# Batch 2's second MLP product: a third quad of half-size products, and four products of each quad added alone

## The chip, the core and the metric

The kernel runs on one core of a Trainium2 chip. Its engines run side by side and each works through its own instructions in order: TensorE (PE) multiplies matrices into PSUM, ScalarE (ACT) and VectorE (DVE) read PSUM and write SBUF, GpSimd (POOL) works on SBUF and issues many of the loads, SyncE (SP) issues the stores and the transposing DMAs. Semaphores hold an instruction back until what it reads is written and what it overwrites has been read. The metric is the device time of one run in microseconds, smaller being better.

## The reference

Block-sparse attention over 4 batches, 8 heads, 768 tokens and 64 columns a head, and then a residual MLP block of width 512 on the result:

```python
scores = (q @ k^T) / 8, masked by blocks of 32      # attn = softmax(scores) @ v
x  = attn, heads side by side                       # 4 x 768 x 512
u  = x + lam * (w_tok @ (alpha1 * x + beta1))       # mixes tokens
a2 = alpha2 * u + beta2
out = u + lam * (relu(a2 @ w_ch1) @ w_ch2)          # 512 -> 2048 -> 512
```

The last line has the first MLP product (to 2048 hidden columns), the relu, and the second MLP product (back to 512 columns). The change is in how the second product of batch 2 is computed.

## The kernel before

The 16 pairs of heads (four in each batch) go through attention one after the other; each pair has nine units of 128 keys by up to 512 queries for both key blocks. For a unit PE makes the scores (line 605), ACT the exponential (623), DVE multiplies by the mask (640, `emit_keep`), PE multiplies by the values (675), and at the end of a head DVE divides by the sums (692, 693). POOL, for a few heads DVE, then forms `alpha1 * x + beta1` (709, 710, `emit_a1pp`). When two pairs are through, PE mixes their tokens (`job_tok2`, 850), DVE adds the result to x (862), and transposing DMAs on SP's queue (`emit_udma`) turn it for the MLP. When a batch is complete its MLP follows, woven into the attention of the next batch.

The first MLP product of a batch is 32 jobs (`job_f1`, 923): each makes 128 hidden columns for 384 tokens (half c of the batch) with four matmuls, and ACT writes the relu (930). The second product works on six tiles of 128 tokens. In batches 0 and 1 a tile takes four "g" jobs (`job_f2`, 1075), each of four matmuls of 512 columns, into one PSUM tile, and one add of 512 columns by DVE (1084). In batch 3 and, for some tiles, in batch 2, tiles t and t + 3 are taken together as a quad: a 2 x 2 block product in which seven half-size products (eight matmuls of 256 columns each, `job_p` and `mul`, 1189) stand for eight. For that DVE first forms sums of blocks of the weights (`job_t`) and, for every quad, four sums of hidden blocks ("S" jobs, `job_s`, 1162); afterwards it adds the products into x (`plus`, 1199). In batch 2, tiles 0 and 3 are done straight with eight g jobs, and t = 1, 2 are quads. In a quad of the version before, products 1, 6 and 5 pile up in one PSUM tile and 7 and 4 in another, and DVE adds the tile after each. The last batch has its first product in a similar form: "M" jobs (`job_m`, 1036), for which sums of weights ("W" jobs, `job_w`, 986) and of inputs ("D" jobs, `job_d`, 1001) are formed by DVE.

Nothing is reordered by a planner: the order in which instructions are issued is the order on each engine. For the first 45 units it comes from `PLAN`: a job stands at unit int(when), before or after that unit's other work, by the fraction (`fns`). After that it comes from the strings W1, W2, W2L and W3. Each string of the first three is a third of a pair, and each letter a job, taken from the front of its list: q scores of three units and the first exponential, x an exponential, k a masking multiply, p a block of the value product, f a first-product job, g a second-product job (the quads' products too), T token mixing, S a sum for a quad, W and D the sums for the last batch, a the a1pp of pair 15's first head, d a transposing DMA, Y, K, Q, L copies and loads. The strings of W2L (lines 69 to 80) hold pairs 12 to 15; W3 (83 to 86) the rest.

[...] A first-product job, a token-mixing job, a third of the score tiles, a straight tile and most half-size products each take an "mm" tile. Each new one gets the buffer that was given back first, and its first matmul waits until the engine that empties that buffer is done:

```python
def mm_tile(shape=(P, DM), dt=FP):
    return psum.tile(list(shape), dt, name="mm", tag="mm", bufs=3)
```

Of the kernel before, what the change touches and what calls it, by code (L numbers as in the profile page):

```python
# [66 lines left out]
]  # L67
W2L = [
# [12 lines left out]
]  # L81
W3 = [
# [4 lines left out]
]  # L87
STR = (2, 3)
HN = NH // 2
HC = DM // 2  # L90
FW = 6
FIRST = [
    (0, 1), (0, 2), (1, 1), (1, 2), (0, 6), (2, 1), (1, 6), (2, 2), (0, 5), (0, 7),
    (1, 5), (1, 7), (0, 3), (2, 6), (1, 3), (0, 4), None, None, None, (1, 4),
# [65 lines left out]
    "tok0_1": 16.29,  # L160
    "tok0_2": 17.09,
    "tok0_3": 18.68,
    "loadq4": 18.7,
    "lv3": 19.01,
    "loadk4": 19.19,
    "tok0_4": 19.61,
    "mask5": 20.08,
    "mask9": 20.29,
    "tq3": 20.7,
    "tok0_5": 20.76,  # L170
    "loadv5": 20.77,
    "loadq5": 21.09,
    "tk3": 22.44,
    "loadk5": 22.78,
    "udma0": 23.28,
# [77 lines left out]
def kernel(  # L253
# [211 lines left out]
    def sp_tile():  # L465
        return psum.tile([P, 2, 512], FP, name="sp", tag="sp", bufs=2)
# [6 lines left out]
    def mm_tile(shape=(P, DM), dt=FP):  # L473
        return psum.tile(list(shape), dt, name="mm", tag="mm", bufs=3)

    def op_tile(shape):
        phase["op"] += 1
        if phase["first"] and phase["op"] % 2 == 0:
            return mm_tile(shape)
        return psum.tile(shape, FP, name="op", tag="op", bufs=1)  # L480
# [434 lines left out]
    def h_row(b, c, n):  # L915
        if (b, c) not in hts:
            hts[(b, c)] = ap_.tile([P, NH, QC], BF, name="hts", tag="hts", bufs=2)
        return hts[(b, c)][:, n, :]

    def job_f1(b, c, n):  # L920
        ps = mm_tile()
        for dk in range(4):
            nc.tensor.matmul(  # L923
                ps[:, 0:QC],
                w1b[:, dk, ts(n, P)],
                uTs[b][:, dk, ts(c, QC)],
                start=(dk == 0),
                stop=(dk == 3),
            )
        nc.scalar.activation(h_row(b, c, n), ps[:, 0:QC], AF.Relu)  # L930
        did.add(("f", b, c, n))

    wsum, usum = [], []
# [194 lines left out]
    )  # L1128

    xs = {}  # L1130

    def a_of(b, t, name, r=slice(0, HN)):
        if name in ("X1", "X2"):
            return xs[(b, t, name)][:, r]
        c, half = {"11": (0, 0), "12": (0, 1), "21": (1, 0), "22": (1, 1)}[name]
        return hts[(b, c)][:, HN * half + r.start : HN * half + r.stop, ts(t, P)]

# [7 lines left out]
    def job_s(b, t, n, r=slice(0, HN)):  # L1145
        dst, a, c, op = SOP[n]
        relu_late()
        rows = range(r.start, r.stop)
        for name in (a, c):
            if name[0] == "X":  # L1150
                assert all(("S", b, t, int(name[1]), m) in did for m in rows)
            else:
                h, half = divmod(int(name) - 11, 10)
                assert all(("f", b, h, HN * half + m) in did for m in rows)
        if n == 3:
            assert all(("S", b, t, 1, m) in did for m in rows)
        if n == 4:
            assert (b, t, 2) in did
        if dst[0] == "X" and (b, t, dst) not in xs:
            tag, bufs = ("eT", 6) if b == B - 1 else ("xs", 4)  # L1160
            xs[(b, t, dst)] = ap_.tile([P, HN, P], BF, name="xs", tag=tag, bufs=bufs)
        nc.vector.tensor_tensor(
            out=a_of(b, t, dst, r), in0=a_of(b, t, a, r), in1=a_of(b, t, c, r), op=op
        )
        did.update(("S", b, t, n, m) for m in rows)
# [12 lines left out]
    def mul(b, t, n, ps, start, cols=slice(0, HC), rows=slice(0, HN)):  # L1178
        a, m, need = PROD[n]
        assert m in bq or all((m, r) in did for r in range(0, HN, 2))  # L1180
        if need:
            assert all(("S", b, t, need, r) in did for r in range(HN))
        ends = (0, HN - 1)
        c, half = {"1": (0, 0), "X": (1, 0)}.get(a[0], (1, 0))
        if need == 0:
            h, half = divmod(int(a) - 11, 10)
            assert all(("f", b, h, HN * half + r) in did for r in range(rows.start, rows.stop))
        for r in range(rows.start, rows.stop):
            nc.tensor.matmul(  # L1189
                ps,  # L1190
                a_of(b, t, a)[:, r],
                b_rows(m, r)[:, 0, cols],
                start=(start and r == ends[0]),
                stop=(r == ends[1]),
                skip_group_check=True,
            )
# [4 lines left out]
    def twice(ps):  # L1201
        return ps.unsqueeze(1).broadcast_to([P, 2, HC])

    lo, hi = slice(0, HC), slice(HC, DM)

    def job_p(b, t, n, rows=slice(0, HN)):
        x = x_sbs[b]
# [86 lines left out]
    def start_mlp(b):  # L1294
        if b == B - 1:
            todo["f"] += [
                lambda j=j: job_m(*j) if len(j) == 2 else job_f1(*j) for j in last_f1()
            ]
        else:
            todo["f"] += [  # L1300
                lambda c=c, n=n: job_f1(b, c, n) for c in range(2) for n in range(NH)
            ]
        if b not in STR:
            todo["g"] += [
                lambda o=o, g=g: job_f2(b, o, g) for o in range(NT) for g in range(4)
            ]
            return
        todo["g"] += [
            lambda j=j: job_f2(b, *j[:2]) if j[-1] == "g" else job_p(b, *j)
            for j in P_ORDER[b]  # L1310
        ]
        todo["S"] += [lambda t=t, n=n, r=r: job_s(b, t, n, r) for t, n, r in S_ORDER[b]]

    REST = (6, 7, 5, 4, 3)
    P_ORDER = {
        2: [(0, g, "g") for g in range(4)]
        + [(t, 2) for t in (1, 2)]
        + [(3, g, "g") for g in range(4)]
        + [(t, 1) for t in (1, 2)]
        + [(t, n) for t in (1, 2) for n in REST],  # L1320
        3: [(0, 1, slice(r, r + 2)) for r in (0, 2, 4)]
        + [(1, 1), (0, 1, slice(6, HN)), (2, 1)]
        + [(t, 2) for t in range(2)]
        + [(t, n) for t in range(2) for n in REST]
        + [(2, n) for n in (2,) + REST],
    }
    ALL, R1, R2 = slice(0, HN), slice(0, HN // 2), slice(HN // 2, HN)
    S_ORDER = {
        2: [(t, n, ALL) for t in (1, 2) for n in (1, 2, 3, 4)],
        3: [(0, n, r) for r in (R1, R2) for n in (1, 2)]  # L1330
        + [(0, n, ALL) for n in (3, 4)]
        + [(t, n, ALL) for t in (1, 2) for n in (1, 2, 3, 4)],
# [237 lines left out]
```

## Time and profile before

| | us |
|---|---|
| median of three runs (297.27 to 297.41) | 297.3 |
| profiled execution | 297.57 |
| its span | 295.9 |
| PE busy | 289.2 |
| DVE busy | 240.6 |
| ACT busy | 217.0 |
| POOL busy | 110.1 |

The profile is of one execution. Its page begins with each engine's busy time and its share of the span; below stand 40 slices of the span, 7.4 us each, with a digit for the busy share in tenths, 9 being 90% or more. Other views show instructions in order of time with start, duration, engine, line of the kernel, operation, what it writes from what it reads, and in brackets the idle time before it and what ended it; groups of equal instructions with their count and mean; the chain of work that ended last; and the busy time of each engine in a stretch. The ends of matmuls are modelled: their starts are what counts.

### The profile page before, as it was taken

The numbers are of one execution on the slowest core, as the hardware profiler recorded it, in microseconds if no ns is written. First come the engines' busy times: TensorE is split into PE (matmuls) and PEld (weight loads), VectorE is DVE, ScalarE is ACT, GpSimd is POOL, SyncE is SP. The second block draws the span as 40 slices with busy tenths as digits, with TensorE's granted clock in tenths as the row PEclk, the third lists the DMA queues.
The fourth block names the chain that finished last, engine by engine and source line by source line (L and its number), as shares of the span: only waits on it lengthen the run. The fifth ranks groups of instructions, "written<-read, shape, count | busy, mean of one in ns | idle before, by whom it ended". The sixth has DMA issues, their size and how long they took to land.

```text
span 295.9 us, 7583 instructions
## 1 busy us (share of the span) xinstructions
PE 289.2 (98%) x3097; PEld 192.7 (65%) x3097; DVE 240.6 (81%) x498; ACT 217.0 (73%) x324; POOL 110.1 (37%) x149
## 2 busy tenths in 40 slices
PE   7999999999999999999999999999999999999995
PEld 2678878665467565565576556465567678766884
DVE  4988899995668887988758788795946999999894
ACT  5999989999799872999779780899869764477000
POOL 8997978632343720347321450335320300000000
PEclk9999999999999999999999999999999999999999
DMA  6999999981392996737962957653520214400023
GB/s 176 204 198 167 193 158 204 177 143 27 95 143 60 106 190 103 109 75 98 122 122 57 142 77 161 91 123 44 96 62 2 53 38 20 151 1 3 0 91 124
DMA packets 57274, 31.09 MB, mean 105 GB/s; under 512 B 37204, under 2 KB 54016, under 8 KB 57240
## 3 DMA queue, kind: packets, MB, share of 16 engines
q0 software_dynamic: 16752, 14.22, 33.6%
q1 hardware_dynamic: 40020, 15.92, 28.2%
q8 instruction: 24, 0.39, 0.6%
q10 hardware_dynamic: 468, 0.47, 0.6%
q14 instruction: 10, 0.08, 0.1%
HBM read 29.75 MB, written 6.29 MB: 122 GB/s over the span
## 4 chain that ended last, share of the span: by engine, by line
PE 84%; DVE 5%; ACT 4%; DMA 4%; issue 1%; POOL 1%; POOLq 0%
PE mm L923 20%; PE mm L1075 16%; PE sp L605 8%; PE op L675 8%; PE mm L850 8%; PE mm L1189 5%; ACT eT L623 4%; PE mm L605 3%; DMA kr<-in_k_dram 3%; PE sp L1189 3%; PE sp L1036 3%; PE mm L1036 3%; PE op L652 2%; PE mm L826 2%; DVE eT L640 1%; DMA x_sb<-in_q_dram 1%
## 5 line engine op out<-in xcount | busy, mean ns | idle before, releaser
L623 ACT ACTIVATE eT<-sp,expb 128x1024 f16<-128x1024 f32 x111 | 118.4, 1118 | 2.4 <-PE sp L605 1.8
L640 DVE TENSOR_TENSOR eT<-eT,mask 128x1024 f16<-128x1024 f16 x99 | 80.1, 835 | 14.2 <-ACT eT L623 14.0
L709 POOL TENSOR_TENSOR a1pp<-x_sb,vbc 128x384 bf16<-128x384 f32 x25 | 28.5, 1139 | 119.2 <-DVE x_sb L693 84.6
L923 PE MATMUL mm<-uT,w1b 128*128 128x384 bf16 x384 | 70.6, 326 | 0.1
L623 ACT ACTIVATE eT<-mm,expb 128x512 f16<-128x512 f32 x66 | 41.7, 684 | 26.6 <-PE mm L605 26.3
L1075 PE MATMUL mm<-w2b,hts 128*128 128x512 bf16 x224 | 54.7, 380 | 0.0
L930 ACT ACTIVATE hts<-mm 128x384 bf16<-128x384 f32 x96 | 45.1, 501 | 10.1 <-PE mm L923 9.5
L923 PEld LDWEIGHTS <-w1b 128*128 128x128 bf16 x384 | 35.6, 98 | 23.9 <-issue 2.4
L675 PEld LDWEIGHTS <-eT 128*128 128x128 f16 x792 | 29.8, 98 | 8.5 <-issue 1.7
L1075 PEld LDWEIGHTS <-hts 128*128 128x128 bf16 x224 | 19.8, 98 | 22.3 <-issue 3.9
L675 PE MATMUL op<-vext,eT 128*128 128x65 f16 x792 | 32.2, 194 | 0.0
L605 PE MATMUL sp<-qTs,kTs 88*128 88x512 bf16 (+1 forms) x120 | 27.0, 325 | 1.3 <-ACT eT L623 0.7
L710 POOL TENSOR_TENSOR a1pp<-a1pp,vbc 128x384 bf16<-128x384 bf16 x25 | 26.9, 1075 | 2.0
L850 PE MATMUL mm<-a1pp,wtokT 128*128 128x256 bf16 x216 | 25.9, 273 | 0.1
L850 PEld LDWEIGHTS <-wtokT 128*128 128x128 bf16 x216 | 20.6, 98 | 5.6 <-issue 1.8
L1189 PEld LDWEIGHTS <-hts 128*128 128x128 bf16 x208 | 19.6, 98 | 3.3 <-issue 0.3
L862 DVE TENSOR_TENSOR x_sb<-x_sb,mm 128x512 f32<-128x512 f32 x18 | 12.3, 684 | 9.9 <-PE mm L850 9.8
L605 PE MATMUL sp<-qhT,khT 64*128 64x256 bf16 (+1 forms) x176 | 19.8, 322 | 0.0
L605 PEld LDWEIGHTS <-khT 64*128 64x128 bf16 x264 | 10.6, 94 | 12.7 <-issue 9.2
L652 PEld LDWEIGHTS <-eT 128*128 128x128 f16 x360 | 14.9, 98 | 3.8 <-issue 0.3
L1084 DVE TENSOR_TENSOR x_sb<-x_sb,mm 128x512 f32<-128x512 f32 x14 | 9.6, 685 | 8.8 <-PE mm L1075 8.7
L693 DVE TENSOR_TENSOR x_sb<-op,rcp 128x384 f32<-128x384 f32 x28 | 15.6, 557 | 1.0
(137 smaller groups left out, 395.2 us busy)
## 6 DMA issues: line engine op xcount, KB each, us to landing
out_dram<-x_sb SPq DMA_DIRECT2D x23, 256.0 KB
qpad<-in_q_dram POOLq DMA_DIRECT2D x15, 192.0 KB, 4.5
kr<-in_k_dram POOLq DMA_DIRECT2D x15, 192.0 KB, 5.3
vr<-in_v_dram POOLq DMA_DIRECT2D x15, 192.0 KB, 5.9
w1b<-in_moe_w_ch_dram POOLq DMA_DIRECT2D x4, 512.0 KB, 9.8
w2b<-in_moe_w_ch_dram POOLq DMA_DIRECT2D x4, 512.0 KB, 8.5
hts<-in_moe_w_tok_dram POOLq DMA_DIRECT2D x2, 576.0 KB, 8.9
x_sb<-in_k_dram ACTq DMA_DIRECT2D x2, 192.0 KB
```

The costliest lines, as they stand in the source:

```text
L605: nc.tensor.matmul(sp[jj][:, dst], lhsT, rhs, start=True, stop=True, skip_group_check=True,)
L623: nc.scalar.activation(dst, at, AF.Exp, bias=expb[:], scale=SCALE)
L640: nc.vector.tensor_mul(out=e, in0=e, in1=keep)
L652: nc.tensor.matmul(op[0][:, o, :], ets[u][:, jj, h * QB + n * P : h * QB + n * P + P], vexts[i % NVB][:, w, 2 * jp + jj, :], start=op[1] == 0,
L675: nc.tensor.matmul(op[0][:, o, :], ets[u][:, jj, h * QB + n * P : h * QB + n * P + P], vexts[i % NVB][:, w, 2 * jp + jj, :], start=op[1] == 0,
L709: eng.tensor_tensor(out=dst, in0=x_sbs[b][:, :, cols], in1=bc[0], op=ALU.mult)
L710: eng.tensor_tensor(out=dst, in0=dst, in1=bc[1], op=ALU.add)
L850: nc.tensor.matmul(ps[:, o], wtokT[:, os_, ts(2 * n + o, P)], a1pps[i][:, os_, :], start=(os_ == 0 and o == 0), stop=(os_ == NT - 1 and o ...
L923: nc.tensor.matmul(ps[:, 0:QC], w1b[:, dk, ts(n, P)], uTs[b][:, dk, ts(c, QC)], start=(dk == 0), stop=(dk == 3),)
L930: nc.scalar.activation(h_row(b, c, n), ps[:, 0:QC], AF.Relu)
L1075: nc.tensor.matmul(ps[:], ht[:, nk, ts(o % 3, P)], w2b[:, nk, :], start=(nk == 0), stop=(nk == NH - 1),)
L1189: nc.tensor.matmul(ps, a_of(b, t, a)[:, r], b_rows(m, r)[:, 0, cols], start=(start and r == ends[0]), stop=(r == ends[1]), skip_group_chec ...
```

## The change

Batch 2's second product now has three quads (t = 0, 1, 2) and no straight tile. They go through a new function, `job_pi`: products 1, 2, 4 and 7 each take an "mm" tile of their own and are added to every block of x that needs them (product 1 to all four, 7 to two); only 6, 5 and 3 pile up in one tile. Most sums are formed in two halves (R1 and R2), and the first-product jobs of the batch's second half go in the order 0, 8, 1, 9, ... so that both halves of the hidden columns grow together. The relu of one of them, (2, 1, 1), moves from ACT to DVE. Quad 2's sums lie in buffers that held keys and values. The strings are written anew to fit. In the first part the loads of queries and keys of pair 4 and of queries of pair 5 stand earlier in `PLAN`, and one transposing DMA (the second d of line 70) stands one string earlier. Cut to its core:

```diff
 W2L = [
     "q 0 p p g k x L x p f k 1 K 2 k",
-    "q Q 0 g x g f v v s T T x k 1 k p p g g T g g Y d 2 k",
-    "q g 0 k g d 1 2 p x k g x k",
+    "q Q 0 g x g f v v s T T x k 1 k p p g g T g g Y d d 2 k",
+    "q g 0 k g 1 2 p x k g x k",
     "q 0 p k x v Q v 1 2 p k x g k g",
     "q 0 p 1 g x k f K k x f p p k 2 f",
     "q k 0 f x f p s f f x 1 L p k 2 f f f k Y f",
-    "q f L f 0 f k W W W W W W W W 1 f Y x f p g x f p f g k k 2",
-    "q x k x k Q 0 g 1 s f f g p 2 p f f k p f",
-    "q T 0 k f 1 x k f T x f 2 p k K p f",
-    "q x 0 x T k 1 k f 2 k f Q f d p L",
-    "q x 0 x K k g d k s f g f 1 k p p S S g 2",
-    "q p Y x x k g k S 0 1 k 2 g v g v g",
+    "q f L f 0 f k W W W W W W W W 1 f Y x f p g x f p f g k k 2 f",
+    "q x k x k Q 0 g 1 s f p f p 2 g f f k p f",
+    "q S S S S S S T 0 k f 1 x k f T x f 2 p k K p f",
+    "q S S S S x 0 x T k 1 k f 2 k f Q f d p L",
+    "q x 0 x K k g d k s f g 1 k p p S S S S g 2",
+    "q p Y x x k g k S 0 1 k a S 2 g v g v",
 ]
 W3 = [
-    "a p p p g s g g T S T S T S S S d g g U g v g D g D D g D g D g D D",
-    "f f f W W f W W f f f f f W f f f f f W f f f f f f f W f f",
-    "W f f f f f f f f f f f f f f f S f f f f S f f f f f f f f f g f f f g f g g f",
+    "p p p g g s g g T S T S T S S d g g U g v S g D g S S D D g D D g D D",
+    "f f f f W f f W f f W f f W f f f f f f W f f f f f f f f f",
+    "f W f f f f f f f W f f f f f S f f W f f S f f f f f f f f f g f f f g f g g f",
     "g S S g g S g S g S g S g S g S g g S g S g S g g g S g g g g g",
 ]
...
+HALVES = [n // 2 + HN * (n % 2) for n in range(NH)]
+ON_DVE = [(2, 1, 1)]
...
-    "loadq4": 18.7,
+    "loadq4": 15.391,
-    "loadk4": 19.19,
+    "loadk4": 15.495,
-    "loadq5": 21.09,
+    "loadq5": 20.705,
...
-        nc.scalar.activation(h_row(b, c, n), ps[:, 0:QC], AF.Relu)
+        if (b, c, n) in ON_DVE:
+            nc.vector.tensor_scalar_max(out=h_row(b, c, n), in0=ps[:, 0:QC], scalar1=0.0)
+        else:
+            nc.scalar.activation(h_row(b, c, n), ps[:, 0:QC], AF.Relu)
...
+        if dst[0] == "X" and (b, t) == SPLIT:
+            xs[(b, t, dst, r.start // R2.start)] = ap_.tile(
+                [P, HN // 2, P], BF, name="xs", tag="kr" if n == 1 else "vr", bufs=2
+            )
...
+    def job_pi(b, t, n):
+        x = x_sbs[b]
+        quad = x[:, t : t + 4 : 3].rearrange("p a (h c) -> p a h c", h=2)
+        if n == 6:
+            banks[(b, t)] = (sp_tile()[:, 0] if t < 2 else op_tile([P, DM])[:])[:, lo]
+        chained = n in (6, 5, 3)
+        ps = banks[(b, t)] if chained else mm_tile()[:, lo]
+        mul(b, t, n, ps, n not in (5, 3))
+        if n == 1:
+            plus(quad, ps.unsqueeze(1).unsqueeze(1).broadcast_to([P, 2, 2, HC]))
+        elif n == 7:
+            plus(quad[:, 1], twice(ps))
+        else:
+            plus(quad[:, int(n in (4, 6, 5)), int(n in (3, 5))], ps)
+        did.add((b, t, n))
+        for o, uses in ((t + 3, (1, 4, 6, 7, 5)), (t, (1, 2, 5, 3))):
+            if n in uses and all((b, t, m) in did for m in uses):
+                emit_store(b, o, slice(0, DM))
...
     P_ORDER = {
-        2: [(0, g, "g") for g in range(4)]
-        + [(t, 2) for t in (1, 2)]
-        + [(3, g, "g") for g in range(4)]
-        + [(t, 1) for t in (1, 2)]
-        + [(t, n) for t in (1, 2) for n in REST],
+        2: [(0, 1), (0, 2), (1, 1), (2, 1), (1, 2), (2, 2)]
+        + [(0, 4), (1, 4), (2, 4), (0, 6), (1, 6), (0, 7), (0, 5), (1, 7)]
+        + [(1, 5), (0, 3), (2, 6), (1, 3), (2, 5), (2, 7), (2, 3)],
...
     S_ORDER = {
-        2: [(t, n, ALL) for t in (1, 2) for n in (1, 2, 3, 4)],
+        2: [(t, n, R1) for t in range(3) for n in (1, 2, 3)]
+        + [(0, 4, R1)]
+        + [(t, n, R2) for t in range(2) for n in (1, 2)]
+        + [(0, 3, R2), (1, 3, R2), (0, 4, R2)]
+        + [(1, 4, ALL), (2, 1, R2), (2, 2, R2), (2, 3, R2)]
+        + [(2, 4, r) for r in (R1, R2)],
```

More of the change, by code (lines that the diff above doesn't have):

```diff
@@ L1130 @@
     xs = {}
+    ALL, R1, R2 = slice(0, HN), slice(0, HN // 2), slice(HN // 2, HN)
+    SPLIT = (B - 2, 2)
     def a_of(b, t, name, r=slice(0, HN)):
         if name in ("X1", "X2"):
-            return xs[(b, t, name)][:, r]
+            if (b, t) != SPLIT:
+                return xs[(b, t, name)][:, r]
+            n, h = r.start // R2.start, R2.start
+            return xs[(b, t, name, n)][:, r.start - h * n : r.stop - h * n]
         c, half = {"11": (0, 0), "12": (0, 1), "21": (1, 0), "22": (1, 1)}[name]
@@ L1158, in job_s @@
             assert (b, t, 2) in did
-        if dst[0] == "X" and (b, t, dst) not in xs:
+        if dst[0] == "X" and (b, t) == SPLIT:
+            xs[(b, t, dst, r.start // R2.start)] = ap_.tile(
+                [P, HN // 2, P], BF, name="xs", tag="kr" if n == 1 else "vr", bufs=2
+            )
+        elif dst[0] == "X" and (b, t, dst) not in xs:
             tag, bufs = ("eT", 6) if b == B - 1 else ("xs", 4)
@@ L1190, in mul @@
                 ps,
-                a_of(b, t, a)[:, r],
+                a_of(b, t, a, slice(r, r + 1))[:, 0],
                 b_rows(m, r)[:, 0, cols],
@@ L1300, in start_mlp @@
             todo["f"] += [
-                lambda c=c, n=n: job_f1(b, c, n) for c in range(2) for n in range(NH)
+                lambda c=c, n=n: job_f1(b, c, n)
+                for c in range(2)
+                for n in (HALVES if b in STR and c == 1 else range(NH))
             ]
@@ L1308, in start_mlp @@
         todo["g"] += [
-            lambda j=j: job_f2(b, *j[:2]) if j[-1] == "g" else job_p(b, *j)
-            for j in P_ORDER[b]
+            lambda j=j: (job_p if b == B - 1 else job_pi)(b, *j) for j in P_ORDER[b]
         ]
@@ L1326 @@
     }
-    ALL, R1, R2 = slice(0, HN), slice(0, HN // 2), slice(HN // 2, HN)
     S_ORDER = {
-        2: [(t, n, ALL) for t in (1, 2) for n in (1, 2, 3, 4)],
+        2: [(t, n, R1) for t in range(3) for n in (1, 2, 3)]
[4 more added lines that the diff above has]
+        + [(2, 4, r) for r in (R1, R2)],
         3: [(0, n, r) for r in (R1, R2) for n in (1, 2)]
```

## The prediction

> **What bounds the kernel now.** I read the page's busy shares and slices first, then a table by stretch, then single instructions in order of time. Strings of the written order are named by their line in the kernel (line 75 is the seventh of W2L); a sum of the S jobs is a "sum", "DVE" is VectorE, "PE" TensorE, "ACT" ScalarE, "POOL" GpSimd.
>
> ```profile
> PE 289.2 (98%) x3097; PEld 192.7 (65%) x3097; DVE 240.6 (81%) x498; ACT 217.0 (73%) x324; POOL 110.1 (37%) x149
> PE   7999999999999999999999999999999999999995
> DVE  4988899995668887988758788795946999999894
> ```
>
> PE is full from end to end, so any wait put into it lengthens the run. DVE has room on average, but from slice 31 on (about 229 us) it is nearly full too. The stretches are those of the strings at lines 75 and 79, and of the last batch's first MLP product:
>
> ```profile
> 203.66:211.53 7.87, 7.87 (x69) 4.48 (x70) 6.06 (x14) 6.75 (x12) 1.97 (x3) 1.00 0.83 129
> 229.77:235.63 5.86, 5.74 (x64) 3.85 (x62) 5.61 (x10) 4.56 (x8) 2.25 (x2) 1.00 0.35 67
> 255.34:274.22 18.88, 18.88 (x121) 11.59 (x119) 18.01 (x58) 13.85 (x32) 0.00 (x0) 1.00 0.08 30
> ```
>
> After the length come PE, weight loads, DVE, ACT, POOL. The string at 75 leaves DVE 1.8 us, the one at 79 only 0.25, the long stretch 0.87 of 18.88.
>
> How can DVE hold PE up? The "mm" PSUM tile has three buffers, taken in turn. In order of time, with start and duration:
>
> ```profile
> 230.60 1.05 PE L1189 MATMUL mm<-w2b,hts 128*128 128x256 bf16 x8
> 231.48 0.81 PE L923 MATMUL mm<-uT,w1b 128*128 128x384 bf16 x4
> 231.49 1.41 DVE L640 TENSOR_TENSOR eT<-eT,mask 128x1024 f16<-128x1024 f16 x1 [0.21 <-ACT eT L623]
> 232.13 1.04 PE L1189 MATMUL mm<-w2b,hts 128*128 128x256 bf16 x8
> 232.82 0.41 DVE L1199 TENSOR_TENSOR x_sb<-x_sb,mm 128x256 f32<-128x256 f32 x1
> 233.16 1.08 DVE L640 TENSOR_TENSOR eT<-eT,mask 128x1024 f16<-128x1024 f16 x1
> 233.29 0.81 PE L923 MATMUL mm<-uT,w1b 128*128 128x384 bf16 x4
> 234.49 0.68 DVE L640 TENSOR_TENSOR eT<-eT,mask 128x1024 f16<-128x1024 f16 x1
> ```
>
> Three tiles are taken from 230.60 to 232.13; the fourth needs the first one's buffer. A product takes 0.87 (next fence), so PE was ready at 233.00; it started at 233.29, just after the add at 232.82 + 0.41 = 233.23 had emptied that buffer. The add was late because a masking multiply stood before it on DVE. This wait of 0.29 is what the change makes more of.
>
> **PE work.** From the chain of waits, start and length:
>
> ```profile
> 208.20 0.86 PE mm L1075 x4
> 213.32 1.30 PE mm L923 x8
> 222.01 1.31 PE mm L850 x12
> 253.86 1.75 PE mm L1189 x16
> ```
>
> Tiles 0 and 3 cost eight chunks of 0.86, 6.88 us; their quad costs seven products of 1.75 / 2 = 0.875, 6.12. PE saves **0.76**. A first-product job (f1) takes 0.65, a token-mixing job of the last pairs 1.31.
>
> **DVE work.** Groups by form, busy time and mean ns from 180 us on:
>
> ```profile
> L1052 DVE TENSOR_TENSOR hts<-mm,part 128x384 bf16<-128x384 f32 x24 | 13.1, 551 | 0.7 <-PE mm L1036 0.5
> L1199 DVE TENSOR_TENSOR x_sb<-x_sb,mm 128x256 f32<-128x256 f32 x15 | 6.1, 415 | 0.9 <-PE mm L1189 0.7
> L1019 DVE TENSOR_SCALAR hts<-hts 128x384 bf16<-128x384 bf16 x24 | 5.8, 249 | 0.0
> L1162 DVE TENSOR_TENSOR hts<-hts 128x1024 bf16<-128x1024 bf16 x5 | 3.4, 683 | 0.0
> L1199 DVE TENSOR_TENSOR x_sb<-x_sb,sp 128x512 f32<-128x512 f32 x4 | 2.7, 682 | 0.5 <-PE sp L1189 0.5
> L1162 DVE TENSOR_TENSOR xs<-hts 128x512 bf16<-128x512 bf16 x2 | 0.8, 421 | 0.0
> ```
>
> Product 1, added alone, goes to four blocks, 128x1024. No row has that add. Its bounds are 0.68 (the bf16 sum of that size, SBUF only) and 1.36 (two adds of 512); 415 ns at 256 and 682 at 512 give 1.04 ns an element, so 1.21 us is my estimate, from the rows of the same kind. A quad's adds come to 1.21 + 5 x 0.415 + 0.68 = 3.97; before, 6 x 0.415 + 0.68 = 3.17, and a straight pair 2 x 0.68. Three quads are 11.9 against 7.7: +4.2. The sums were 8 x 0.68 = 5.5 and become 22 x 0.42 + 0.68 = 9.9: +4.4. One relu comes from ACT: it reads PSUM, so between L1019's 0.25 and L1052's 0.55; nearer the second, which reads PSUM too, 0.5. Together DVE gets some **9 us** more, nearly all of it in the strings 75 to 80. What counts is where PE needs a buffer that DVE has not emptied.
>
> *String 75*, in order of time:
>
> ```profile
> 205.44 0.69 DVE L640 TENSOR_TENSOR eT<-eT,mask 128x1024 f16<-128x1024 f16 x1 [1.84 <-ACT eT L623]
> 206.05 1.96 DVE L986 TENSOR_TENSOR wsum<-w1b 128x768 bf16<-128x768 bf16 x4
> 208.86 1.02 DVE L986 TENSOR_TENSOR wsum<-w1b,wsum 128x768 bf16<-128x768 bf16 x2
> 209.80 0.35 DVE L333 COPY vext<-vr 128x768 f16<-128x768 f16 x1
> 210.12 0.20 DVE L692 RECIPROCAL rcp<-op 128x6 f32<-128x6 f32 x1
> 210.57 1.03 PE L1075 MATMUL mm<-w2b,hts 128*128 128x512 bf16 x4
> 210.83 2.08 DVE L640 TENSOR_TENSOR eT<-eT,mask 128x1024 f16<-128x1024 f16 x2
> 211.00 1.36 POOL L709 TENSOR_TENSOR a1pp<-x_sb,vbc 128x384 bf16<-128x384 f32 x1 [5.56 <-DVE x_sb L693]
> 211.53 0.39 PE L605 MATMUL mm<-qhT,khT 64*128 64x512 bf16 x2
> 212.28 1.04 PE L1075 MATMUL mm<-w2b,hts 128*128 128x512 bf16 x4
> 212.44 1.25 POOL L710 TENSOR_TENSOR a1pp<-a1pp,vbc 128x384 bf16<-128x384 bf16 x1
> ```
>
> In the places of the two straight chunks stand products 1 and 2 of quad 0; product 2, due at 210.57, is the third tile after product 1 and needs its buffer. DVE works without a gap from 205.44 to 210.12, through the eight weight sums (L986) and the copy. Only then comes product 1's add: to 211.33. PE waits **0.8** and starts at 211.4. The reciprocal and multiply that stood at 210.12 take 0.71, to 212.0; product 2's add must wait until 211.4 + 1.05 = 212.45 and ends at 212.85. Then two masking multiplies, then the relu of f1 (1, 1). The multiplies took 2.08 here, under POOL's two a1pp operations at 211.00 and 212.44, which follow DVE's multiply and so move along with it; alone they are 0.68 each (234.49). So the relu ends between 212.85 + 1.3 + 0.25 = 214.4 and 212.85 + 2.1 + 0.55 = 215.5.
>
> Next in PE's order are f1 (1, 1) to 212.3 + 0.65 = 212.9, the score matmuls (0.75, from 211.53 to 212.28), and at 213.7 product 1 of quad 1, three tiles after that f1: it needs the relu's buffer. The wait is 0.7 to 1.8; I take **1.1**. Behind it, in PE's order, stand all later products and the scores that ACT waits for.
>
> [...]
>
> *String 77*. Six half sums now stand before the first token-mixing add. They can begin when the last f1 of string 76 has its relu, some 0.7 after the string's start, and take 6 x 0.42 = 2.5; the add (0.68) ends at 3.9. The second token-mixing job, again three tiles on, is due at 0.75 + 1.31 + 1.30 = 3.4. Wait 0.5; 1.2 if POOL's pair lies over the sums as over the multiplies, 0 if they overlap fully: **0.5**.
>
> *Strings 79, 80*. DVE is done with the multiplies at 234.49 + 0.68 = 235.17, then four half sums (4 x 0.42, to 236.8), then product 4 of quad 0's add, to 237.2. Product 4 of quad 1 needs its buffer. PE's order up to there: from 231.48 an f1 0.65, product 0.87, two key blocks 0.7, product 0.87, scores 0.75, a key block 0.36: due at 235.7. Wait **1.45**, 0.3 less if POOL lets the 1.41 multiply through.
>
> The 0.29 above falls away, and a wait of some 0.2 before the last token mixing, since PE comes later there:
>
> ```profile
> 244.18 3.83 PEld L850 LDWEIGHTS <-wtokT 128*128 128x128 bf16 x36 [0.35 <-DVE a1pp L710]
> ```
>
> That is **-0.5**. The operands of pair 15's a1pp are issued 1.1 earlier and the two adds behind them later: counted in the order above.
>
> **The loads.**
>
> ```profile
> 24.07 0.72 POOL L322 DMA_DIRECT2D vr<-in_v_dram  x1
> 29.05 8.63 DMA kr<-in_k_dram
> 24.00:38.00 14.00, 13.65 (x223) 10.95 (x221) 12.76 (x28) 13.76 (x14) 11.48 (x19) 1.00 1.21 175
> 37.73 0.51 PE L515 MATMUL mm<-ident,kr 128*128 128x128 bf16 x6 [0.35 <-DMA kr<-in_k_dram]
> ```
>
> PE waits 0.35 for pair 4's keys, issued at 29.05, landed at 37.68. They would be issued some 3.5 sooner, right after the values (24.07). But the DMA engines are full all this time (share 1.21), and the weights, values and queries that are ahead of the keys stay ahead of them, only the last two exchanged. So 0 to -0.35; I take **-0.1**. POOL's later work moves forward by the two issues, 1.4 us, and waits for nothing new. The moved transpose passes one output store on SP's queue and costs nothing; no one waits for it long. The later weight sums have over ten products of 0.33 before their use. The new sums' buffers last held keys and values of pairs that are through. All three: 0; if the cover were gone, some tenths.
>
> **Sum.** 0.8 + 1.1 + 0.5 + 1.45 = 3.85 of new waits; -0.76 of work; -0.5 of old waits; -0.1: **+2.5**. The profiled execution took 297.57 (span 295.9), 0.27 over the median of 297.30. It would be 300.1, the median **299.8**.
>
> **Rivals.** (A) The forecast; with each term at its ends, 297.3 + 0.8 + 0.7 + 0 + 1.15 - 0.76 - 0.5 - 0.35 = 298.3 and 297.3 + 0.8 + 1.8 + 1.2 + 1.45 - 0.76 - 0.5 = 301.3. (B) Slower still: the DVE arrears reach the last batch, where DVE has 0.87 us of room in 18.88. With the upper ends and 0.8 more there, 302.1. For it: the adds of that stretch hold the same three buffers. Against: the end of string 83 leaves DVE room to catch up. (C) Faster: PE does not stand behind the adds, because buffers come free in another order than in turn. Then 0.76 + 0.5 + 0.1 are gained, 295.9; one wait of 0.8 may remain, 296.7. It decides as soon as the new waits stay under 0.8 in all. For it: PE shows such a wait only once now. Against: the 233.29 row. (D) No change: every unknown is at its cheapest. With an add of 0.68 product 2 of quad 0 waits 0.25; with POOL yielding and a relu of 0.25 the next wait stays 0.7, the third is 0, the last 1.15, and the keys' wait goes: 2.1 - 0.76 - 0.5 - 0.35 = +0.5, 297.8. For it: DVE operations in a row overlap a little (233.16 against 233.23). Against: all must fall well together.
>
> **Numbers.** A 0.58, B 0.17, C 0.14, D 0.11: slower 0.75, same 0.11, faster 0.14. 0.2%, 0.6 us, is about what a measurement can tell here. The range, 296.6 to 301.4, takes in A, D and the upper end of C; A's own is 298.3 to 301.3.
>
> **What would show it.** Right: product 2 of quad 0 and product 1 of quad 1 begin just after a DVE add and a DVE relu end, PE gaps of 0.8 and about 1.1 there, one near 1.4 before quad 1's product 4; PE's first 35 us unchanged; the keys' wait still there. Wrong: PE without gaps from 203 to 245, a 128x1024 add much under 1.2, or the relu done before the scores that follow it.

## The result and the profile after

The changed kernel takes **299.68 us** (median of seven runs, 299.14 to 302.25) beside 297.30 for the kernel before: 1.0087 times as long, 95% interval 1.0069 to 1.0105. Run again beside the kernel before, it took 299.64 against 297.37, 1.0076 (1.0063 to 1.0088). So it loses some 2.3 us.

The first profile of the changed kernel is of the longest of its seven executions, 302.25 us; what is read below comes from a second profile, of an execution of 299.39 us with a span of 297.4. (In the first, PE stood 1.39 us before pair 4's keys and 1.22 inside a value product at 52.31; neither is in the second.) From its page, busy times and slices:

```profile
PE 288.4 (97%) x3105; PEld 195.5 (66%) x3121; DVE 249.0 (84%) x519; ACT 216.8 (73%) x323; POOL 109.0 (37%) x149
...
PE   7999999999999999999999999999998999999995
...
DVE  4988899985588796978778777986998999899994
```

DVE has 249.0 us of work where it had 240.6. (PE's busy time is short by some records; its starts are used instead.) The same table by stretch as before the change, from the string at line 75 to the first sum of the last batch, for the changed kernel in its second profile and then, some rows of it, for the kernel before. After the length come PE, weight loads, DVE, ACT, POOL:

```profile
202.83:211.38 8.55, 8.55 (x82) 5.66 (x82) 6.73 (x14) 6.77 (x12) 1.57 (x3) 1.00 0.95 142
211.38:219.37 7.99, 7.47 (x81) 5.14 (x82) 7.77 (x11) 5.13 (x8) 2.10 (x2) 1.00 0.01 2
219.37:227.64 8.27, 6.97 (x73) 4.86 (x73) 7.75 (x17) 5.02 (x8) 1.97 (x2) 1.00 0.01 3
...
232.13:237.07 4.94, 4.94 (x64) 3.86 (x62) 4.70 (x9) 4.07 (x7) 2.25 (x2) 1.00 0.41 80
237.07:258.46 21.39, 20.75 (x219) 17.35 (x219) 20.09 (x48) 9.87 (x16) 0.00 (x0) 1.00 0.19 60
sum 55.63, PE 53.18 PEld 39.95 DVE 50.62 ACT 35.25 POOL 7.89; mean PE 8.86 PEld 6.66 DVE 8.44 ACT 5.88 POOL 1.32
```

```profile
211.53:218.47 6.94, 6.94 (x73) 4.07 (x74) 4.86 (x7) 5.01 (x8) 2.08 (x2) 1.00 0.22 58
218.47:225.29 6.82, 6.82 (x74) 4.88 (x74) 4.36 (x10) 4.90 (x8) 1.91 (x2) 1.00 0.06 11
...
sum 53.08, PE 52.89 PEld 37.26 DVE 42.60 ACT 35.47 POOL 8.20; mean PE 8.82 PEld 6.21 DVE 7.10 ACT 5.91 POOL 1.37
```

The loss is here: 55.63 against 53.08, 2.55 us, and 0.15 in the last batch. DVE's work rises from 42.60 to 50.62. The strings at 75 and 79 only exchange a first-product job (8.55 for 7.87, 4.94 for 5.86, with the old wait of 0.29 gone); the string at 76 grows by 1.05 and that at 77 by 1.45, both by waits:

```profile
209.24 1.22 DVE L1213 TENSOR_TENSOR x_sb<-x_sb,mm 128x1024 f32<-128x1024 f32 x1
209.76 1.04 PE L1203 MATMUL mm<-w2b,hts 128*128 128x256 bf16 x8
...
212.54 1.03 PE L1203 MATMUL mm<-w2b,hts 128*128 128x256 bf16 x8 [0.20 <-ACT eT L625]
...
214.03 0.55 DVE L933 TENSOR_SCALAR hts<-mm 128x384 bf16<-128x384 f32 x1
...
214.63 0.81 PE L925 MATMUL mm<-uT,w1b 128*128 128x384 bf16 x4
...
215.70 2.34 DVE L1213 TENSOR_TENSOR x_sb<-x_sb,mm 128x1024 f32<-128x1024 f32 x2
216.96 1.46 PE L925 MATMUL mm<-uT,w1b 128*128 128x384 bf16 x8 [0.28 <-DVE x_sb L1213]
...
219.76 0.99 POOL L711 TENSOR_TENSOR a1pp<-x_sb,vbc 128x384 bf16<-128x384 f32 x1 [6.20 <-PE mm L607]
...
220.00 1.03 DVE L1176 TENSOR_TENSOR xs<-hts 128x512 bf16<-128x512 bf16 x1 [0.39 <-ACT hts L935]
...
220.83 0.98 POOL L712 TENSOR_TENSOR a1pp<-a1pp,vbc 128x384 bf16<-128x384 bf16 x1
221.06 1.02 DVE L1176 TENSOR_TENSOR xs<-xs,hts 128x512 bf16<-128x512 bf16 x1
...
222.01 0.41 DVE L1176 TENSOR_TENSOR hts<-hts 128x512 bf16<-128x512 bf16 x1
...
223.47 0.68 DVE L864 TENSOR_TENSOR x_sb<-x_sb,mm 128x512 f32<-128x512 f32 x1
...
224.20 1.47 PE L852 MATMUL mm<-a1pp,wtokT 128*128 128x256 bf16 x12 [1.29 <-DVE x_sb L864]
...
239.04 0.41 DVE L1213 TENSOR_TENSOR x_sb<-x_sb,mm 128x256 f32<-128x256 f32 x1
...
239.51 1.03 PE L1203 MATMUL mm<-kTs,hts 128*128 128x256 bf16 x8 [0.24 <-DVE x_sb L1213]
...
242.68 0.54 PE L677 MATMUL op<-vext,eT 128*128 128x65 f16 x12 [0.40 <-DVE eT L642]
```

The brackets count from the modelled end of the matmul before; a wait is given here as the time from start to start over what that step takes elsewhere, which is mostly 0.1 to 0.2 more. Product 2 of quad 0 (209.76) starts in the middle of the add of product 1 (209.24 to 210.46), so it does not use that product's buffer, and waits for nothing. Product 1 of quad 1 (212.54) waits 0.40 for an exponential: it starts 1.16 after the first score matmul, where 0.76 is usual (the expectations below give 0.36). Two first-product jobs behind it wait 0.21 for the relu on DVE (to 214.58) and 0.44 for the first of two four-block adds (to 216.91). The second token mixing of the string at 77 waits 1.46 for its add, which stands behind the six sums. In the strings at 79 and 80, product 4 of quad 2 waits 0.40, and two blocks of a value product wait 0.12 and 0.56 for masking multiplies. With 0.14 just ahead of the last batch that is 3.73 us; 0.51 of old waits are gone, and PE's work is shorter by what remains, 3.73 - 0.51 - 2.55 = 0.67.

### The profile page after: what moved, and what is told of

It is laid out like the page before. It is cut to its first block, busy times and chain, and to the rows that moved or that the text cites. A ratio compares the mean times of both kernels' runs of the same rounds, so it can differ in the third digit from the quotient of the medians.

```text
span 300.3 us, 7657 instructions
## 1 busy us (share of the span) xinstructions
PE 290.2 (97%) x3121; PEld 195.7 (65%) x3121; DVE 249.5 (83%) x519; ACT 216.8 (72%) x323; POOL 109.0 (36%) x149
## 4 chain that ended last, share of the span: by engine, by line
PE 81%; DVE 9%; DMA 4%; ACT 3%; issue 1%; POOL 0%; DVEq 0%
PE mm L925 18%; PE mm L1080 14%; PE sp L607 8%; PE op L677 7%; PE mm L852 7%; DMA kr<-in_k_dram 4%; PE mm L1203 4%; PE sp L1203 3%; PE mm L607 3%; DVE eT L642 3%; PE sp L1041 3%; PE mm L1041 3%; ACT eT L625 2%; PE op L1203 2%; PE op L654 2%; PE mm L828 1%
## 5 line engine op out<-in xcount | busy, mean ns | idle before, releaser
L1080 PE MATMUL mm<-w2b,hts 128*128 128x512 bf16 x192 | 46.8, 380 | 0.0
L1080 PEld LDWEIGHTS <-hts 128*128 128x128 bf16 x192 | 16.9, 98 | 19.4 <-issue 3.6
L1203 PEld LDWEIGHTS <-hts 128*128 128x128 bf16 x248 | 23.2, 98 | 4.7 <-issue 1.2
L607 PE MATMUL sp<-qhT,khT 64*128 64x512 bf16 (+1 forms) x176 | 19.9, 322 | 0.0
L864 DVE TENSOR_TENSOR x_sb<-x_sb,mm 128x512 f32<-128x512 f32 x18 | 12.3, 684 | 5.7 <-PE mm L852 5.7
L1089 DVE TENSOR_TENSOR x_sb<-x_sb,mm 128x512 f32<-128x512 f32 x12 | 8.2, 685 | 8.2 <-PE mm L1080 8.1
## 6 DMA issues: line engine op xcount, KB each, us to landing
w1b<-in_moe_w_ch_dram POOLq DMA_DIRECT2D x4, 512.0 KB, 11.9
```

The lines of the kernel that those rows point to most:

```text
L607: nc.tensor.matmul(sp[jj][:, dst], lhsT, rhs, start=True, stop=True, skip_group_check=True,)
L1080: nc.tensor.matmul(ps[:], ht[:, nk, ts(o % 3, P)], w2b[:, nk, :], start=(nk == 0), stop=(nk == NH - 1),)
L1203: nc.tensor.matmul(ps, a_of(b, t, a, slice(r, r + 1))[:, 0], b_rows(m, r)[:, 0, cols], start=(start and r == ends[0]), stop=(r == ends[1]) ...
```

## The experiments

All ratios are against the kernel before, run beside each kernel.

**The changed kernel once more.**

> The changed kernel once more, for a second profile. Its first profile is of an execution of 302.25 us, 2.6 over the median of 299.68; in it the string at line 75 began at 205.72, 2.07 us later than before (203.66). Theory 'one execution': the 1.39 us before pair 4's keys and the 1.22 us inside a value product at 52.31 belong to that execution; the string at 75 then begins at 203.7 (203.2 to 204.2) here, the span is about 297.7 and the loss against before lies from 205 to 260. Rival 'the loads': the two waits come each time, the string begins at 205 or later again, and the execution is as long as the first or the later strings are 2 us shorter than there. The waits of 1.46 (token mixing in the string at 77) and 0.40 (products in the string at 79) are expected in both.

299.64 us, 1.0076 (1.0063 to 1.0088). The string at 75 began at 202.83, a little ahead of the 203.2 to 204.2 that was expected, and neither of the two waits came: 'one execution' holds. The late start of the first profile says nothing about the change.

**The loads alone**, in the kernel before:

```diff
-    "loadq4": 18.7,
+    "loadq4": 15.391,
-    "loadk4": 19.19,
+    "loadk4": 15.495,
-    "loadq5": 21.09,
+    "loadq5": 20.705,
```

> The kernel before, with the three new places of the loads (queries and keys of pair 4, queries of pair 5) and nothing else. As predicted (the queue of transfers is full, the keys stay behind the same others): 0 to 0.35 us shorter, 297.2, with the wait for pair 4's keys 0.1 to 0.5 us as before. Rival (the first profile after: keys issued 3.4 us sooner landed 1.1 us later): 0.9 to 2.1 us longer, 298.2 to 299.4, with a wait of about 1.4 before the keys.

296.91 us, 0.9983 (0.9975 to 0.9992): 0.46 shorter. The rival falls, and the gain is a little more than the 0.35 that bounded it.

**The change without the loads**, the same three lines turned back in the changed kernel.

> The changed kernel with the three loads where they stood before, so the quads, the sums, the relu on DVE and the moved transpose alone. As predicted: 299.8, the same as the changed kernel within 0.3, since the loads were put at -0.1. Rival (the loads cost 0.9 to 2.1): 297.6 to 298.8.

299.97 us, 1.0081 (1.0069 to 1.0093), 0.33 over the changed kernel, by intervals that overlap. As predicted, but only the run before shows a gain clear of its noise, and the profiled execution is here as long as the changed kernel's (299.37 and 299.39). How the loads gain isn't settled. In order of time, the transposes of pair 4's keys, ahead of which PE waited in the kernel before, with the loads alone and then in the changed kernel with the old places:

```profile
37.41 0.50 PE L515 MATMUL mm<-ident,kr 128*128 128x128 bf16 x6
```

```profile
36.93 0.50 PE L517 MATMUL mm<-ident,kr 128*128 128x128 bf16 x6
```

From the view of the keys' tile, the times from issue to landing of the keys issued around them, again with the loads alone and then with the old places:

```profile
DMA to landing us min/median/max: 5.6/11.1/11.3
```

```profile
DMA to landing us min/median/max: 4.7/6.5/7.6
```

Keys that are issued sooner took longer to land (median 11.1 against 6.5), as predicted; in the changed kernel and in the kernel before the medians are 8.9 and 8.6, so two executions alone don't say by how much. And no bracket stands behind either transpose: with the old places too there was no wait, so the one of the kernel before doesn't come in each execution.

**Buffers in turn.** The three mm tiles get a tag each, and a list says which one a new tile takes: the one that was given back first.

```diff
+MM_ORDER = (
...
+    "0210210210210210210210210210210210210210210210210210210210212021"
+    "202120112102"
+)
...
     def mm_tile(shape=(P, DM), dt=FP):
-        return psum.tile(list(shape), dt, name="mm", tag="mm", bufs=3)
+        tag = "mm" + MM_ORDER[len(used)]
+        used.append(tag)
+        return psum.tile(list(shape), dt, name="mm", tag=tag, bufs=1)
```

> The changed kernel with the three mm buffers handed out strictly in turn of their giving back, as the prediction assumed; in the changed kernel 53 of the last 65 tiles lie in another buffer than that. Theory 'buffers': the predicted waits come back. Product 2 of quad 0 waits about 0.7 for the four-block add, product 1 of quad 1 waits 0.7 to 1.8 for the relu on DVE, product 4 of quad 1 about 1.4; the changed kernel has 0, 0.36 and 0.40 in their places. The kernel is 1 to 3 us longer than the changed one, 300.7 to 302.7. Rival 'DVE's load alone': which buffer is taken does not matter because DVE's work must be done anyway before the next string; the waits move and the time stays at 299.7 within 0.5.

300.84 us, 1.0117 (1.0101 to 1.0132), 1.2 over the changed kernel. In its profile, in order of time:

```profile
209.59 1.22 DVE L1224 TENSOR_TENSOR x_sb<-x_sb,mm 128x1024 f32<-128x1024 f32 x1
...
210.86 1.03 PE L1214 MATMUL mm<-w2b,hts 128*128 128x256 bf16 x8 [0.59 <-DVE x_sb L1224]
...
214.38 0.54 DVE L944 TENSOR_SCALAR hts<-mm 128x384 bf16<-128x384 f32 x1
...
214.98 1.03 PE L1214 MATMUL mm<-w2b,hts 128*128 128x256 bf16 x8 [1.68 <-DVE hts L944]
...
240.90 0.41 DVE L1224 TENSOR_TENSOR x_sb<-x_sb,mm 128x256 f32<-128x256 f32 x1
...
241.37 1.80 PE L1214 MATMUL mm<-kTs,hts 128*128 128x256 bf16 x15 [1.14 <-DVE x_sb L1224]
```

The three waits of the prediction are there, each behind the DVE instruction that it named: 0.75 for the four-block add (to 210.81), 1.76 for the relu (to 214.92), 1.30 for the add of quad 0's product 4 (to 241.31), and the waits of 0.21, 0.44, 0.40, 0.12 and 0.56 are gone. Theory 'buffers' holds. The waits of this kernel, with 1.52 in the string at 77 and 0.14, come to 5.47 against 3.73, 1.74 more; from the string at 75 to the last batch this execution is 1.60 longer, and the medians differ by 1.2.

**The six sums behind the token mixings:**

```diff
-    "q S S S S S S T 0 k f 1 x k f T x f 2 p k K p f",
+    "q T 0 k f 1 x k f T S S S S S S x f 2 p k K p f",
```

> The changed kernel with the six half sums of the string at line 77 behind both token mixings of that string, in place of ahead of the first. In the second profile after the change the second token mixing waits 1.46 there, for an add that stands behind these six sums on DVE (220.00 to 223.47). Theory 'order on DVE': the add is done by about 222.2, the wait is 0.2 or less and the kernel is 1.2 to 1.5 us shorter than the changed one (299.65), 298.2 to 298.5. Rival 'DVE's load': DVE is busy for 7.75 of the 8.27 us of that string, so the six sums only hold up something later, masking multiplies or the add of the string at 78; half the wait or more comes back there and the time is 299.0 or more.

299.04 us, 1.0061 (1.0049 to 1.0073): 0.6 shorter. The wait of 1.46 is gone and the string at 77 takes 6.82 again, but in the string at 78 a new one has come:

```profile
229.61 0.42 DVE L1176 TENSOR_TENSOR hts<-hts,xs 128x512 bf16<-128x512 bf16 x1
...
229.95 0.68 DVE L864 TENSOR_TENSOR x_sb<-x_sb,mm 128x512 f32<-128x512 f32 x1
...
230.68 0.81 PE L925 MATMUL mm<-uT,w1b 128*128 128x384 bf16 x4 [0.89 <-DVE x_sb L864]
```

The string's own four sums now stand between the delayed DVE and its add; PE waits 1.06. The rival, DVE's load, had the better of it.

**Products exchanged**, so that the four-block adds are apart:

```diff
-        2: [(0, 1), (0, 2), (1, 1), (2, 1), (1, 2), (2, 2)]
+        2: [(0, 1), (0, 2), (1, 1), (1, 2), (2, 1), (2, 2)]
```

> The changed kernel with products 2 of quad 1 and 1 of quad 2 exchanged, so that the four-block adds (1.21 us each) of quads 1 and 2 are no longer in a row on DVE. In the second profile after the change they run as a pair at 215.70 for 2.34 us and an f1 right behind waits 0.44 for the second. Theory: that wait goes to 0 to 0.1 and the one before the products in the string at 79 (0.40) grows by no more than 0.2, since a 1.21 add now lies there in place of one of 0.41: 299.2 to 299.5. Rival: the four-block add costs more where it is moved to, DVE being busy for 4.70 of 4.94 us there: 0.8 more, 300.0 to 300.4.

300.18 us, 1.0099 (1.0086 to 1.0113): 0.5 longer, and the rival is right. The first-product job still waits 0.44. It waits for the first of the two adds, not for the second: in the second profile of the changed kernel it starts at 216.96, 0.05 after 215.70 + 1.21. My reading had taken the pair as one. In the string at 79, where the 1.21 add now lies, there is a new wait of 0.34.

**All relus on ACT:**

```diff
-ON_DVE = [(2, 1, 1)]
+ON_DVE = []
```

> The changed kernel with the relu of f1 (2, 1, 1) on ACT as all others. As predicted (the relu on DVE stands behind masking multiplies and holds a buffer): the wait of 0.36 ahead of product 1 of quad 1 goes or falls to 0.1, DVE has 0.55 less: 0.2 to 0.5 us shorter, 299.2 to 299.5. Rival: the relu comes first on ACT and puts the exponentials of the string at 76 back by 0.5 (ACT has them in a row, 211.80 to 215.08); the wait in question ends with one of these exponentials (0.20 by the row), so it grows: 0.2 to 0.6 us longer, 299.9 to 300.3.

298.94 us, 1.0060 (1.0047 to 1.0073): 0.7 shorter, more than expected. The waits of 0.40, 0.21 and 0.44 make place for one of 0.38. With the relu elsewhere the program also hands out its mm buffers otherwise from there on, so the two causes, DVE's 0.55 us and the buffers, aren't told apart here.

**The three together.**

> The three edits together: sums behind the token mixings, products exchanged, relu on ACT. If the waits are each other's independent causes the gains add up: -1.35 for the sums, -0.25 for the exchange, -0.35 for the relu, 297.7 (297.3 to 298.2), about the time before. Rival 'DVE's load': DVE has 50.6 us of work in the 55.6 from the string at 75 to the last batch against 42.6 of 53.1 before, so the waits move and only half is won: 298.7 or more.

298.93 us, 1.0059 (1.0047 to 1.0070): no more than the relu alone gives, and within the rival's numbers. But the three edits alone had measured 0.6 shorter, 0.5 longer and 0.7 shorter, 0.8 shorter in all, and together they are 0.7 shorter: what failed is the size expected of the single gains (1.35, 0.25 and 0.35), not their adding up.

**Without masking multiplies:**

```diff
-        if i < MP:
+        if i < MP or i >= NPAIR - 2:
             return
```

> The changed kernel without the 18 masking multiplies of pairs 14 and 15 (left out, so these two pairs attend to every key block): DVE loses some 16 to 20 us of work from the string at line 75 on, PE's and ACT's work stays. Theory 'DVE's load': the new waits of the changed kernel (3.85 us from 211 to 260) are all DVE's arrears; they go, but for 0.2 to 0.4, and what is left is the saving that the quads have on PE, 0.76, and the two old waits: 295.9 to 296.6, below the kernel before (297.3) by 0.7 to 1.4. Rival: part of the waits comes from ACT's exponentials or from the order of the buffers and stays whatever DVE does; at least 1.0 of the waits remain, 297.0 or more.

297.30 us, 1.0004 (0.9995 to 1.0013). From 211.67 to 256.61 DVE has 32.2 us of work where the changed kernel had 43.9 in that stretch. The waits of 0.40, 0.21, 0.44, 0.40, 0.12 and 0.56 are gone, 2.13 us, and the time falls by 2.34. (Here too the buffers are handed out otherwise, which may have a part in it.) But one wait has not moved:

```profile
219.25 1.03 DVE L1176 TENSOR_TENSOR xs<-hts 128x512 bf16<-128x512 bf16 x1 [0.39 <-ACT hts L935]
...
220.09 0.97 POOL L712 TENSOR_TENSOR a1pp<-a1pp,vbc 128x384 bf16<-128x384 bf16 x1
220.32 1.02 DVE L1176 TENSOR_TENSOR xs<-xs,hts 128x512 bf16<-128x512 bf16 x1
...
222.73 0.68 DVE L864 TENSOR_TENSOR x_sb<-x_sb,mm 128x512 f32<-128x512 f32 x1
...
223.47 0.70 PE L852 MATMUL mm<-a1pp,wtokT 128*128 128x256 bf16 x5 [1.30 <-DVE x_sb L864]
```

DVE has nothing to do before these sums (it idles 0.39 until their inputs are there), and still PE waits 1.46. So the changed kernel has waits of two kinds: some 2.1 us that go with DVE's load, and 1.46 by the order alone, the six sums ahead of the add, two of them slowed by POOL. The theory that all were arrears falls, and the rival's bound (at least 1.0 of the waits remain) holds.

**Sums behind everything that PE waits for**, with the relu on ACT:

```diff
-ON_DVE = [(2, 1, 1)]
+ON_DVE = []
...
-    "q S S S S S S T 0 k f 1 x k f T x f 2 p k K p f",
-    "q S S S S x 0 x T k 1 k f 2 k f Q f d p L",
-    "q x 0 x K k g d k s f g 1 k p p S S S S g 2",
-    "q p Y x x k g k S 0 1 k a S 2 g v g v",
+    "q T 0 k f 1 x k f T x f S S S S S S 2 p k K p f",
+    "q x 0 x T k 1 k f S S S S 2 k f Q f d p L",
+    "q x 0 x K k g d k s f g 1 k p p S S g 2",
+    "q p Y x x k g k S S S 0 1 k a S 2 g v g v",
```

> The changed kernel with the relu on ACT, the six and the four half sums of the strings at 77 and 78 behind the token mixings and first-product jobs, and two of the four in the string at 79 put into the next. The relu alone gave 0.7, the six sums alone 0.6 (the rest came back as 1.06 ahead of a first-product job in the string at 78, behind that string's own four sums). Theory 'order on DVE': with these four out of the way too the whole 1.46 is won, and 0.2 to 0.4 of the wait of 0.40 at 79: 299.65 - 0.7 - 1.46 - 0.3 = 297.2 (296.9 to 297.6). Rival 'DVE's load': DVE has 16.0 us of work in the 16.3 that these three strings take without waits, so the sums hold up the masking multiplies and value products behind them: 298.0 to 298.9.

298.29 us, 1.0038 (1.0025 to 1.0051), 1.35 shorter than the changed kernel: within the rival's numbers. The strings at 77 and 78 have no wait now; the one at 76 keeps the 0.37 that the relu on ACT left; in those at 79 and 80 PE waits 0.33, 1.01 and 0.61.

**The same with six casts on ACT:**

```diff
-        copy = nc.scalar.copy if i >= NPAIR - 2 else nc.vector.tensor_copy
+        copy = nc.scalar.copy if i >= NPAIR - 4 else nc.vector.tensor_copy
```

> The same, with the six casts of pairs 12 and 13 after their token mixings (0.295 us each on DVE, 0.40 on ACT) moved to ACT, which is busy for 35 of the 56 us from the string at 75 on. If DVE's load is what is left, its 1.8 us less give another 0.5 to 1.2 over the kernel without this edit; if the order on DVE was all, it gives nothing or loses up to 0.4, since a cast on ACT waits for the add and holds up the exponentials behind it.

299.88 us, 1.0089 (1.0076 to 1.0102): 1.6 longer than without the edit, far outside what either side gave. ACT's casts wait for DVE's adds, and all that is behind them on ACT waits too:

```profile
223.92 0.81 PE L925 MATMUL mm<-uT,w1b 128*128 128x384 bf16 x4
...
225.76 0.71 ACT L871 CAST ubf<-x_sb 128x256 bf16<-128x256 f32 x2 [0.98 <-DVE x_sb L864]
...
226.38 1.10 ACT L625 ACTIVATE eT<-sp,expb 128x1024 f16<-128x1024 f32 x1
...
227.39 0.86 ACT L935 ACTIVATE hts<-mm 128x384 bf16<-128x384 f32 x2
...
227.91 0.37 PE L607 MATMUL mm<-qhT,khT 64*128 64x512 bf16 x1 [1.22 <-ACT hts L935]
```

The relu of the first-product job that ran from 223.92 to 224.73 comes at 227.39, behind a cast that waited for its add until 225.76 and behind an exponential, and PE waits 1.39 for its buffer. An engine with a third of its time free (ACT: busy for 35.25 of 55.63 us in the changed kernel) was no place here for work that stands in front of its queue and waits.

**Adds ahead of sums in the strings at 79 and 80:**

```diff
-    "q x 0 x K k g d k s f g 1 k p p S S g 2",
-    "q p Y x x k g k S S S 0 1 k a S 2 g v g v",
+    "q x 0 x K k g d k s f g 1 k p p g S S 2",
+    "q p Y x x k g k 0 1 k S S S S a 2 g v g v",
```

> The kernel with late sums and the relu on ACT, and in the strings at 79 and 80 the sums behind what PE waits for: product 4 of quad 0 ahead of the two sums of 79, and the four sums of 80 behind that string's last masking multiply. In the kernel without this edit PE waits 1.01 there for an add behind two sums (237.06 to 237.41) and 0.61 for a masking multiply behind three (239.97 to 241.10). Theory 'order on DVE': both fall to 0.2 or less, 298.3 - 1.2 = 297.1, no slower than before. Rival 'DVE's load': DVE has 43.9 us of work from the string at 76 to the last batch, where PE without waits would take 43.4; the sums then hold up the adds and multiplies behind them and at least half comes back: 297.7 to 298.3.

298.41 us, 1.0035 (1.0022 to 1.0049): nothing gained. 1.01 and 0.61 fall to 0.22 each, and a wait of 1.06 stands where the sums are now, before a product whose tile is emptied by the add at 243.60:

```profile
243.60 0.41 DVE L1213 TENSOR_TENSOR x_sb<-x_sb,sp 128x256 f32<-128x256 f32 x1
...
244.06 1.03 PE L1203 MATMUL sp<-qTs,xs 128*128 128x256 bf16 x8 [0.90 <-DVE x_sb L1213]
```

From the string at 76 to the last batch DVE has 42.35 us of work here in 46.50, of which 2.5 are PE's waits; moving its work about in so full a stretch has only moved the wait. So what is left of the loss, 1.1 us, looks like DVE's load; a kernel with less work on DVE and all else the same was not found. The fastest kernel of all is the kernel before with the new loads, 296.91.

## Why the prediction was right, point by point

The forecast was +2.5 us and 299.8; the changed kernel took 299.64 to 299.68. The sum of the new waits, predicted at 3.85, was 3.73. That the two are so near is partly luck: the places differ.

| wait before | predicted | changed kernel | buffers in turn |
|---|---|---|---|
| product 2 of quad 0 | 0.8 | 0 | 0.75 |
| product 1 of quad 1 | 1.1 (0.7 to 1.8) | 0.40 | 1.76 |
| two first-product jobs of the string at 76 | none | 0.65 | 0 |
| second token mixing of the string at 77 | 0.5 (0 to 1.2) | 1.46 | 1.52 |
| product 4 of quad 1 | 1.45 | 0 | 1.30 |
| product 4 of quad 2, value product | none | 1.08 | 0 |
| last products of batch 2 | none | 0.14 | 0.14 |
| sum | 3.85 | 3.73 | 5.47 |

**The step that failed** is "product 2, due at 210.57, is the third tile after product 1 and needs its buffer", and with it "product 1 of quad 1, three tiles after that f1: it needs the relu's buffer" and "Product 4 of quad 1 needs its buffer". In the kernel before, tiles took their buffers in turn wherever it mattered, and I carried that over. In the changed kernel 53 of the last 65 mm tiles lie in another buffer than in turn, beginning with product 2 of quad 0. In the program only six tiles depart from the turn, the others follow from these, and all six go the same way: they pass over the buffer that DVE is to empty and take one that ACT empties. Product 2 of quad 0 takes the buffer of a first-product job, whose relu ended at 209.66, in place of that of product 1, whose add ended at 210.46. Which buffer a tile gets is settled when the program is built; why it departs from the turn there no run shows. With the buffers in turn, the three waits came as named, 0.75 for 0.8, 1.76 near the top of its range, 1.30 for 1.45. The observation that rival C rests on, buffers in another order, was thus true, but not its result: the other order saved 1.2 us, not all, since the same late DVE held up other jobs (0.65 and 1.08) and the wait of the string at 77 does not depend on it.

**String 77.** The mechanism was right, its size was not: 1.46 for 0.5, over the upper end of 1.2. The working put six sums at 6 x 0.42; the first two took 1.03 and 1.02, because POOL's a1pp pair lay over them (219.76 to 221.81). The bound had scaled POOL's effect as on the multiplies, 2.08 for 1.36; it was 2.05 for 0.83. A masking multiply under POOL's next pair stands in two other rows of the changed kernel:

```profile
233.72 1.00 POOL L711 TENSOR_TENSOR a1pp<-x_sb,vbc 128x384 bf16<-128x384 f32 x1 [11.91 <-DVE x_sb L695]
233.85 1.42 DVE L642 TENSOR_TENSOR eT<-eT,mask 128x1024 f16<-128x1024 f16 x1 [0.21 <-ACT eT L625]
```

The sums, 0.41 or 0.42 alone, end 0.28 and 0.27 after POOL's instructions, the multiply, 0.68 alone, 0.55 after: each has all but some 0.13 of its own time still to go when POOL ends. So what is lost in these three rows is what is left of POOL's instruction, and not a factor: the two sums lost 0.61 and 0.60, the multiply 0.74, and with 1.2 more the term would have been 1.7, nearer to the 1.46 measured. In all three POOL had begun first, and its instructions took 0.99, 0.98 and 1.00; where a multiply had begun first, at 210.83 in the kernel before, it took its 0.68 and POOL's instruction (211.00) 1.36. That DVE's multiplies get through at POOL's cost, as the prediction's lower ends and rival D have it, did not come: the two ahead of the relu took 2.71 (from 211.40) where they had taken 2.08, the one of the string at 79 1.42 for 1.41.

**The other terms.** DVE's load: 8.0 us more (42.60 to 50.62) for "some 9". Its parts, by groups of equal form from the string at 75 to the first sum of the last batch, two rows of the changed kernel:

```profile
L1213 DVE TENSOR_TENSOR x_sb<-x_sb,mm 128x1024 f32<-128x1024 f32 x3 | 3.6, 1213 | 0.0
...
L933 DVE TENSOR_SCALAR hts<-mm 128x384 bf16<-128x384 f32 x1 | 0.5, 545 | 0.0
```

The four-block add was estimated at 1.21 and took 1.213. The relu was put at 0.5 and took 0.545, the upper bound. The adds of three quads come to 11.8 us (11.9 predicted), the sums to 11.0 (9.9; the 1.2 that POOL adds is the difference). PE's work fell by 0.67, the remainder above, for 0.76 predicted; old waits by 0.51 for 0.5. The loads alone gave 0.46 for 0.1. The relu on DVE was costed as one wait of 1.1; undoing it, which also changes the buffers, gave 0.7. Rival B, arrears into the last batch, did not come: only 0.15 us more are lost there. Rival D, all unknowns at their cheapest, fails already on the string at 77, 1.46 for 0.

Of the signs that the prediction gave, a PE gap before product 2 of quad 0 and one near 1.4 before product 4 of quad 1 did not show, product 1 of quad 1 began after an exponential and not after the relu, and the keys' wait was gone. By the first of these alone the forecast would have looked wrong. It held because it rested on DVE's arrears, and those meet PE at one buffer or at another.

## What to carry to other kernels

When an engine beside the bound one goes from 80% to 91% of a stretch (42.6 of 53.1 us to 50.6 of 55.6), count on its arrears reaching the bound engine, and don't count on winning a named wait whole by moving work about: a kernel that removed 1.46 of named waits got 0.6 and one that removed 1.18 got nothing, the rest coming back a string further on. A wait by order alone is told from one by load by taking other work off the engine: what stays, as the 1.46 did, comes from the order. Which buffer of a pool a tile gets is part of the program, and has to be read anew in the changed program before a wait is put on one instruction.

## What was not expected of the hardware

The half sums (128x512, 0.41 to 0.42 us alone) took 1.02 to 1.03 beside POOL, 2.5 times as long: they end when POOL's instruction has ended and some 0.27 more. One execution of the changed kernel was 2.6 us longer than the median of the same program; its profile, the first, has

```profile
38.81 0.51 PE L517 MATMUL mm<-ident,kr 128*128 128x128 bf16 x6 [1.22 <-DMA kr<-in_k_dram]
...
53.55 0.22 PE L654 MATMUL op<-vext,eT 128*128 128x65 f16 x2 [1.05 <-issue]
```

a late landing of the keys, and a stop of PE in the middle of a value product for nothing that the profile shows. Neither came again in the second profile of that kernel. Without that second profile, 2 of the 4.4 us between the spans before and after would have been laid to the change's loads.
